# Two linear-attention blocks on one core: the key projection by seven products over pairs of token tiles

## The chip, the core and the metric

The kernel runs as one program on one NeuronCore of a Trainium2 chip. The core has five engines, each with its own instruction queue, worked off in order: TensorE (PE in the profile, with its weight loads as PEld) multiplies matrices into PSUM, VectorE (DVE) and ScalarE (ACT) do elementwise work, GpSimd (POOL) does some elementwise work and issues transfers, and SyncE (SP) issues most transfers. PSUM holds eight banks of 128 x 512 fp32. The metric is device time in microseconds of one execution; lower is better.

## The reference

Two independent blocks A and B have the same shapes: x is 2048 x 640, wqkv 640 x 1920, wo 640 x 640, with 32 heads of 20 columns, all fp32. Each block computes

```
q, k, v = split(x @ wqkv)
phi(t)  = where(t > 0, t + 1, exp(t)) + 1e-6
pq, pk  = phi(q), phi(k)
kv = sum over s of pk[s, d] * v[s, e]        (per head)
z  = sum over s of pk[s, d]
o  = (pq @ kv) / (pq . z + 1e-6)
out = o @ wo
```

and the two outputs stand side by side in a 2048 x 1280 result.

## The kernel before

All matrix products run on values split in two: a rounded high part (ScalarE) and the remainder as a low part (VectorE), both in a 32-bit format that TensorE takes at full rate. A product is then three matmuls: high x high, high x low, low x high (`mm3`, L77).

The first half of the program handles 32 token tiles of 128 rows, 16 of each block, in eight groups of four. For a tile, `kmm` (L200) multiplies the transposed tile by wk: five slices of the inner dimension, three matmuls each, two column halves of 320, so 30 matmuls of 128 x 320 into a pair of PSUM banks. `kphi` (L208) makes phi out of it: Exp and Relu on ScalarE straight from PSUM, a combination on VectorE (L219), the high part on ScalarE (L220), the low part on VectorE (L221); GpSimd adds the unsplit value to a running sum in SBUF by an accumulating transfer (L227). After four tiles, `gmm` (L229) sums x^T times pk over the group: ten blocks of 128 x 320, twelve matmuls each, evacuated by VectorE into a running sum (L263, L265). `gmm` of group i runs after tile 4i+5, so the phi of its last tile has a tile and a half of time. The multiplication by wv and wo is moved to small matrices (`kvmm` L305, `mmm` L327), which for each block give one 640 x 640 matrix md.

The second half handles eight units of 512 tokens: `qmm` (L415) makes q transposed, and `outmm` (L525) multiplies the divided phi(q) by md. `outmm` already uses the seven-product scheme: for a pair of token tiles and md cut into a 2 x 2 grid plus a rest, seven products take 18 terms of three matmuls, 54 in place of 60. It needs sums of the left blocks (`d_sums` L479, `d_split` L496) and ten forms of md, made by VectorE (`form_sums1` L358 and after), split (`form_split` L382), stored in DRAM and loaded again.

No scheduler orders the work. The code is written so that instructions come out in order, and a table of slots (`at`, `run`, L85 to L91) hangs side work on named places: ("k", n, c) after slice c of tile n, ("g", i, s) after block s of group i, ("q", u, c, k) and ("o", u, s) in the second half. A low part waits in a list and comes out at the next slot (`flush`, L66).

## Time and profile before

| | |
|---|---|
| median of 3 runs | 585.66 us (585.63 to 586.2) |
| the profiled execution, its own time | 585.71 us |
| span from first to last instruction | 583.9 us |
| PE busy | 577.9 us, 99% |
| DVE busy | 374.4 us, 64% |
| ACT busy | 289.7 us, 50% |
| POOL busy | 68.7 us, 12% |
| granted TensorE clock | 0.999 |
| moved by DMA | 115.97 MB, 199 GB/s on average |

The span is what the trace covers; 1.8 us of the execution lie outside it. "Busy" of PE counts overlapping matmuls once; a single matmul's duration is longer than its share of the time, since matmuls are pipelined, so the time per matmul is read from the chain of waits (duration of a run of matmuls over their count).

### The profile page before, as it was taken

What the parts mean: (1) busy time and instruction counts of PE and PEld (TensorE: products, weight loads), DVE (VectorE), ACT (ScalarE), POOL (GpSimd) and SP (SyncE); (2) the same over time, 40 slices, a digit from 0 to 9 for tenths busy, and PEclk for the clock granted to TensorE, in tenths of its full rate; (3) what the DMA queues carried; (4) which work ended last, traced back from release to release, by engine and by line L of the source; (5) the groups of instructions that cost most, each with busy time, mean ns of one, the idle gap of its engine ahead of it and who ended that gap; (6) DMA issues with size and microseconds to landing.
All of it is one profiled execution on the core that took longest, in us unless ns stands there. A gap on an engine that the chain in (4) does not pass through costs nothing.

```text
span 583.9 us, 9377 instructions
## 1 busy us (share of the span) xinstructions
PE 577.9 (99%) x3620; PEld 549.6 (94%) x3620; DVE 374.4 (64%) x561; ACT 289.7 (50%) x488; POOL 68.7 (12%) x113
## 2 busy tenths in 40 slices
PE   8999999999999999999999999999999999999997
PEld 6999999999999999999998889898998989898897
DVE  5764573635456357476444599968689775757792
ACT  5752634425056175361525766645747455545541
POOL 0120201100011011232100101211011200001010
PEclk9999999999999999999999999999999999999999
DMA  8986864756667659789899795764183996122022
GB/s 285 274 215 191 230 182 111 183 173 187 167 167 193 193 126 263 253 238 299 230 296 270 252 325 182 267 204 171 46 292 100 382 373 203 77 73 91 2 91 90
DMA packets 66897, 115.97 MB, mean 199 GB/s; under 512 B 6372, under 2 KB 29412, under 8 KB 66852
## 3 DMA queue, kind: packets, MB, share of 16 engines
q1 hardware_dynamic: 56708, 82.92, 44.7%
q0 software_dynamic: 10144, 32.45, 20.0%
q8 instruction: 28, 0.46, 0.3%
q14 instruction: 17, 0.14, 0.1%
HBM read 69.47 MB, written 35.39 MB: 180 GB/s over the span
## 4 chain that ended last, share of the span: by engine, by line
PE 98%; DMA 1%; SPq 0%; DVE 0%; issue 0%; ACT 0%; DVEq 0%
PE psk L196 24%; PE pa L549 12%; PE psg L80 8%; PE psg L79 8%; PE psg L78 8%; PE psq L78 8%; PE psq L80 8%; PE psq L79 8%; PE pe L549 6%; PE psb L549 4%; PE pskv L312 2%; DMA wst<-in_A_wk 1%; PE psm L78 1%; PE psm L80 1%; PE psm L79 1%; PE psd L458 0%
## 5 line engine op out<-in xcount | busy, mean ns | idle before, releaser
L80 PE MATMUL psg<-pkh,xnl 128*128 128x320 f32 x320 | 98.9, 309 | 0.0
L79 PE MATMUL psg<-pkl,xnh 128*128 128x320 f32 x320 | 98.9, 309 | 0.0
L78 PE MATMUL psg<-pkh,xnh 128*128 128x320 f32 x320 | 98.9, 309 | 0.0
L78 PE MATMUL psq<-xqh,wqh 128*128 128x512 f32 x200 | 78.6, 393 | 0.0
L80 PE MATMUL psq<-xqh,wql 128*128 128x512 f32 x200 | 78.0, 390 | 0.0
L79 PE MATMUL psq<-xql,wqh 128*128 128x512 f32 x200 | 77.9, 390 | 0.0
L196 PE MATMUL psk<-wkh,xth 128*128 128x320 f32 x320 | 73.9, 312 | 1.1 <-ACT xth L72 1.1
L196 PE MATMUL psk<-wkh,xtl 128*128 128x320 f32 x320 | 73.3, 310 | 0.2 <-DVE xtl L69 0.2
L196 PE MATMUL psk<-wkl,xth 128*128 128x320 f32 x320 | 73.0, 309 | 0.0
L79 PEld LDWEIGHTS psg<-pkl,xnh 128*128 128x128 f32 x320 | 60.1, 188 | 0.0
L80 PEld LDWEIGHTS psg<-pkh,xnl 128*128 128x128 f32 x320 | 60.1, 188 | 0.0
L78 PEld LDWEIGHTS psg<-pkh,xnh 128*128 128x128 f32 x320 | 60.1, 188 | 0.0
L196 PEld LDWEIGHTS psk<-wkh,xth 128*128 128x128 f32 x320 | 53.5, 189 | 2.1 <-ACT xth L72 1.3
L196 PEld LDWEIGHTS psk<-wkh,xtl 128*128 128x128 f32 x320 | 53.7, 189 | 0.5 <-DVE xtl L69 0.5
L196 PEld LDWEIGHTS psk<-wkl,xth 128*128 128x128 f32 x320 | 53.7, 188 | 0.0
L564 ACT ACTIVATE o<-pa 128x320 f32<-128x320 f32 x64 | 27.9, 438 | 45.5 <-PE pa L549 45.3
L219 DVE SCALAR_TENSOR_TENSOR pk<-ek,rk 128x640 f32<-128x640 f32 x32 | 26.4, 825 | 37.1 <-ACT rk L218 36.7
L265 DVE TENSOR_TENSOR gacc<-psg,gacc 128x320 f32<-128x320 f32 (+1 forms) x59 | 28.5, 493 | 32.3 <-PE psg L80 32.3
L437 DVE SCALAR_TENSOR_TENSOR pq<-eq,rq 128x512 f32<-128x512 f32 x40 | 27.6, 690 | 30.5 <-ACT rq L436 30.5
L227 POOL DMA_DIRECT2D zacc<-pk x30 | 25.6, 853 | 174.6 <-DVE pk L219 120.5
L80 PEld LDWEIGHTS psq<-xqh,wql 128*128 128x128 f32 x200 | 37.5, 188 | 7.9
L221 DVE SCALAR_TENSOR_TENSOR pkl<-pk,pkh 128x640 fp32r<-128x640 f32 x32 | 26.4, 826 | 28.7 <-ACT pkh L220 28.7
(122 smaller groups left out, 1203.2 us busy)
## 6 DMA issues: line engine op xcount, KB each, us to landing
xd<-xtl SPq DMA_DIRECT2D x32, 320.0 KB, 3.7
zacc<-pk POOLq DMA_DIRECT2D x32, 320.0 KB, 4.2
xql<-xd SPq DMA_DIRECT2D x40, 256.0 KB, 4.3
out<-o POOLq DMA_DIRECT2D x28, 320.0 KB, 4.2
xns<-in_A_x SPq DMA_DIRECT2D x16, 320.0 KB, 3.2
xts<-in_B_xt_tiles SPq DMA_DIRECT2D x16, 320.0 KB, 3.4
xns<-in_B_x SPq DMA_DIRECT2D x16, 320.0 KB, 3.3
xqs<-in_A_xt SPq DMA_DIRECT2D x20, 256.0 KB, 5.4
```

The costliest lines, as they stand in the source:

```text
L78: nc.tensor.matmul(o, whi, xhi, start=first, stop=False)
L79: nc.tensor.matmul(o, whi, xlo, start=False, stop=False)
L80: nc.tensor.matmul(o, wlo, xhi, start=False, stop=last)
L196: nc.tensor.matmul(ps[:, h, :HF], a[:, c, :], w[:, h * HF:(h + 1) * HF], start=(c == 0 and i == 0), stop=(c == NC - 1 and i == 2))
L219: nc.vector.scalar_tensor_tensor(p.rearrange("p (a b) -> p a b", a=2), e, 1.0, r, op0=OP.min, op1=OP.add)
L221: nc.vector.scalar_tensor_tensor(lo, p, EPS, f32(hi), op0=OP.add, op1=OP.subtract)
L227: nc.gpsimd.dma_start(zacc[b], p, accum_op=OP.add)
L265: nc.vector.tensor_tensor(o, ps, o, op=OP.add)
L312: nc.tensor.matmul(ps[:r, :r].rearrange("p (d h) -> p d h", h=nh), w[:, c, :], gd, start=(c == 0), stop=(c == NC - 1))
L437: nc.vector.scalar_tensor_tensor(pq[u][:, c, :], e, 1.0, r, op0=OP.min, op1=OP.add)
L549: nc.tensor.matmul(ps, x, y, start=start and n == i == 0, stop=n == len(terms) - 1 and i == 2, skip_group_check=True)
L564: copy = lambda x, y: nc.scalar.activation(x, y, AF.Copy)
```

## The change

**Products.** The first three pairs of token tiles (tiles 0 to 5) are multiplied as before (now in `kconv`). From the fourth pair on, x times wk is done for two tiles at once by the seven products of `outmm`, whose tables and evacuation (`STEPS`, `product`, `combine`) are now shared. Pairs number 3 to 15, thirteen in all. Each product accumulates in one of three banks of its pair ("a", "e", "b"); ScalarE copies bank "a" after products 0, 2, 4 and 5 and VectorE adds banks "b" and "e" into the result in SBUF after products 3, 4 and 6. A product that goes on accumulating in a bank has to wait until the copy of it is done.

**Left and right operands.** `x_parts` splits the blocks of x that are used as they are, `x_sums` makes four sums of blocks on VectorE and splits them. Ten forms of wk are made per block: for A on VectorE, kept in SBUF; for B on GpSimd, stored in DRAM and loaded over A's forms (`wform_load`).

**Order.** `both` interleaves the seven products of two pairs, and blocks of the group sum are put between the products of the second. Groups 3 and 7 have one pair, group 4 has three pairs and block A's `kvmm`. `later` and `tick` spread phi over following slots: Exp and Relu, then the combination, the high part, the low part. Exp and Relu now read SBUF.

**GpSimd and DRAM.** The sums and low parts of the forms of md for both blocks, and the low parts of wo for A, move from VectorE to GpSimd. z is summed in two DRAM tiles per block (odd and even token tiles) by accumulating transfers; they are loaded, added on GpSimd (`z_sum`) and multiplied by ones as before. Only the low parts of x that exist are stored for the second half; the others are made there (`round_xq`).

**PSUM.** One pool serves the whole program: three single banks, two "a", two "e", one small.

```diff
+    def bank(name, tag="one"):
+        return psums.tile([P, 512], F32, name=name, tag=tag, bufs={"one": 3, "a": 2, "e": 2, "small": 1}[tag])
...
+    def split(hi, lo, src, now=False, pool=False):
         nc.scalar.activation(hi, src, AF.Copy)
-        lows.append((lo, src, hi))
-        if now:
-            flush()
+        if pool:
+            nc.gpsimd.tensor_tensor(lo, src, f32(hi), op=OP.subtract)
+        elif now:
+            low(lo, src, hi)
+        else:
+            later(1, low, lo, src, hi)
...
+    def x_parts(p, i):
+        r1, r2 = pair_x(p)
+        hi, lo = (kx[0].tile([P, 4, P], F32R, name=f"ka{t}", tag=f"ka{t}{i}", bufs=2) for t in "hl")
+        ka[p, i] = (hi, lo)
+        if i == 0:
+            split(hi, lo, r1[:, 0:4])
+        else:
+            split(hi[:, 0:3], lo[:, 0:3], r2[:, 2:5])
+            split(hi[:, 3], lo[:, 3], r1[:, 4])
+        later(3, store_xt, p, i)
+    def x_sums(p, i):
+        r1, r2 = pair_x(p)
+        a11, a12, a21, a22 = r1[:, 0:2], r1[:, 2:4], r2[:, 0:2], r2[:, 2:4]
+        tt = nc.vector.tensor_tensor
+        if i == 0:
+            t = ks[p, 2] = kx[0].tile([P, 2, 2, P], F32, name="sx", tag="sx", bufs=2)
+            tt(t[:, 0], a21, a22, op=OP.add)
+            tt(t[:, 1], t[:, 0], a11, op=OP.subtract)
+        else:
+            t = ks.pop((p, 2))
+            tt(t[:, 1], a12, t[:, 1], op=OP.subtract)
+            tt(t[:, 0], a11, a21, op=OP.subtract)
+        hi, lo = (kx[0].tile([P, 2, 2, P], F32R, name=f"ks{t}", tag=f"ks{t}{i}", bufs=2) for t in "hl")
+        ks[p, i] = (hi, lo)
+        flat = "p f c s -> p (f c s)"
+        later(1, split, *(x.rearrange(flat) for x in (hi, lo, t)))
...
+    STEPS = [
+        (ksum(A11, 0, 0), "a", True),
+        (ksum(("s", 0, 0), 0, 1), "e", True),
+        (ksum(("s", 0, 1), 2, 0), "a", False),
+        (ksum(A12, 4, 0) + [(A15, 0, (8, 0))], "b", True),
+        (ksum(("s", 1, 0), 2, 1) + [(A25, 0, (8, 1))], "a", False),
+        ([(A22, k, (6, k)) for k in range(2)] + [(A25, 0, (9, 0))], "a", False),
+        (ksum(("s", 1, 1), 4, 1) + [(A15, 0, (8, 1))], "e", False),
+    ]
...
+        terms, where, start = STEPS[n]
+        o = ps[where]
+        for m, ((kind, i, j), k, w) in enumerate(terms):
+            ah, al = (t[:, j + k] if kind == "a" else t[:, j, k] for t in (asum if kind == "a" else ssum)[i])
+            wh, wl = right(*w)
+            for r, (x, y) in enumerate(((ah, wh), (ah, wl), (al, wh))):
+                nc.tensor.matmul(o, x, y, start=start and m == r == 0,
+                                 stop=m == len(terms) - 1 and r == 2, skip_group_check=True)
...
+        if n == 0:
+            copy(t1[:, 0], ps["a"])
+        elif n == 2:
+            copy(t1[:, 1], ps["a"])
+        elif n == 3:
+            plus(t1[:, 0], ps["b"])
+        elif n == 4:
+            copy(t2[:, 1], ps["a"])
+            plus(t2[:, 1], ps["e"])
+        elif n == 5:
+            copy(t2[:, 0], ps["a"])
+        elif n == 6:
+            plus(t1[:, 1], ps["e"])
...
+    def wform(b, i):
+        w = width(i)
+        wf[b, i] = [kx[0].tile([P, w], F32R, name=f"wf{t}{i}", tag=f"wf{t}{i}", bufs=1) for t in "hl"]
+        return wf[b, i]
...
+    def kprod(p, n):
+        b = p // (NT // 2)
+        def right(i, h):
+            if i == 6 or i == 9:
+                return wf[b, i + h]
+            return [t[:, h * HF:(h + 1) * HF] for t in wf[b, i]]
+        if n == 0:
+            kps[p] = {"a": bank("pa", "a")[:, :HF]}
+            kout(p)
+        elif n == 1:
+            kps[p]["e"] = bank("pe", "e")[:, :HF]
+        elif n == 3:
+            kps[p]["b"] = bank("psb")[:, :HF]
+        product(n, kps[p], [ka[p, i] for i in range(2)], [ks[p, i] for i in range(2)], right)
+        combine(n, kps[p], *ko[p])
+        run("p", p, n)
+        if n > 4:
+            kphi(2 * p + 6 - n, ko[p][6 - n])
...
+    def kphi(n, r):
+        b = n // NT
+        e = kg[0].tile([P, 2, HF], F32, name="ek", tag="ek", bufs=3)
+        hi, lo = pk[n] = [kg[0].tile([P, 2, HF], F32R, name=f"pk{t}", tag=f"pk{t}", bufs=6) for t in "hl"]
+        def mix():
+            nc.vector.scalar_tensor_tensor(e, e, 1.0, r, op0=OP.min, op1=OP.add)
+            z = zacc.get((b, n % 2))
+            if z is None:
+                z = zacc[b, n % 2] = dram.tile([P, D], F32, name=f"zd{b}{n % 2}")
+                nc.gpsimd.dma_start(z, e.rearrange("p a b -> p (a b)"))
+            else:
+                nc.gpsimd.dma_start(z, e.rearrange("p a b -> p (a b)"), accum_op=OP.add)
+            later(1, high)
+        def high():
+            nc.scalar.activation(hi, e, AF.Identity, bias=epst)
+            later(1, lowp)
+        def lowp():
+            nc.vector.scalar_tensor_tensor(lo, e, EPS, f32(hi), op0=OP.add, op1=OP.subtract)
+        def start():
+            nc.scalar.activation(e, r, AF.Exp)
+            nc.scalar.activation(r, r, AF.Relu)
+            later(1, mix)
+        if n % 2 or n in (NT - 2, NN - 2):
+            start()
+        else:
...
+    def load_z(b):
+        for t in range(2):
+            wst["z", b, t] = base.tile([P, D], F32, name="zs", tag=f"wo{'hl'[t]}", bufs=2)
+            nc.sync.dma_start(wst["z", b, t], zacc.pop((b, t)))
+    def z_sum(b):
+        x, y = (wst.pop(("z", b, t)) for t in range(2))
+        nc.gpsimd.tensor_tensor(x, x, y, op=OP.add)
+        wst["z", b] = x
...
+        split(*parts, raw.pop((f, b, i))[:, :w], pool=True)
+        fd[f, b, i] = [dram.tile([P, w], F32, name=f"fd{f}{t}{b}{i}") for t in "hl"]
+        for d, t in zip(fd[f, b, i], parts):
             nc.gpsimd.dma_start(d, f32(t))
...
+    def wform_load(i):
+        for d, t in zip(fd.pop(("k", 1, i)), wform(1, i)):
+            nc.sync.dma_start(f32(t), d)
...
+    forms("k", 1, [(0, ("g", 1, 8)), (2, ("p", 5, 1)), (6, ("p", 6, 2)), (4, ("h", 2, 0)), (1, ("g", 2, 0)),
+                   (3, ("g", 2, 2)), (5, ("g", 2, 4)), (7, ("g", 2, 6)), (8, ("g", 2, 8)), (9, ("p", 7, 5))])
+    for i, a in ((0, ("p", 7, 2)), (1, ("p", 7, 2)), (4, ("h", 3, 2)), (5, ("h", 3, 2)), (8, ("h", 3, 2)),
+                 (2, ("h", 3, 3)), (3, ("h", 3, 3)), (6, ("h", 3, 4)), (7, ("h", 3, 4)), (9, ("g", 3, 3))):
+        at(a, wform_load, i)
...
+    at(("p", 9, 2), load_z, 0)
+    at(("kv", 3), z_sum, 0)
+    at(("g", 4, 2), zmm, 0)
+    at(("q", 0, 0, 0), z_sum, 1)
+    at(("g", LG, 7), load_z, 1)
+    at(("q", 0, 1, 0), zmm, 1)
...
+    def both(p, r):
+        prods(p, 0, 1, 3, 2)
+        prods(r, 0)
+        prods(p, 4)
+        prods(r, 1)
+        prods(p, 5)
+        prods(r, 3)
+        prods(p, 6)
+        prods(r, 2)
...
+    for i in range(NU):
+        P0, P1 = 2 * i + 1, 2 * i + 2
+        if i == 0:
+            gsums(i, range(2 * NC), range(4))
+        elif i in (NG - 1, LG):
+            prods(P0, 0, 1, 3, 2)
+            gsums(i, [0], [0, 1])
+            prods(P0, 4)
+            gsums(i, [1], [0, 1])
+            prods(P0, 5, 6)
+            if i == LG:
+                close_pool(kx, "kx")
+                open_pool(q1a, "q1a", "right")
+                open_pool(q1b, "q1b", "right")
+            gsums(i, range(2, 6), [0, 1], {3: "a", 4: "e", 5: "small"})
+            gsums(i, range(6), [3])
+            gsums(i, range(6), [2])
+            gsums(i, range(6, 2 * NC), range(4))
+        elif i == NG:
+            both(P0 - 1, P0)
+            kvs(0)
+            prods(P0, 4)
+            kvs(1)
+            prods(P0, 5, 6)
+            kvs(2, 3, 4, 5)
+            gsums(i, range(3), [0, 1])
+            gsums(i, range(3), [2, 3])
+            gsums(i, [3], range(4))
+            prods(P1, 0, 1, 3, 2)
+            gsums(i, [4], range(4))
+            prods(P1, 4)
+            gsums(i, [5], range(4))
+            prods(P1, 5, 6)
+            gsums(i, range(6, 2 * NC), range(4))
+        else:
+            both(P0, P1)
+            gsums(i, [0], [0, 1])
+            prods(P1, 4)
+            gsums(i, [1, 2], [0, 1])
+            prods(P1, 5, 6)
+            gsums(i, range(3), [2, 3])
+            gsums(i, range(3, 2 * NC), range(4))
```

Three places in the order of instructions matter to the prediction.

First, ScalarE in the first half, around the phi of a tile. Before, for one tile (xnh is the high part of an x tile, ek and rk are Exp and Relu, pkh the high part of phi):

```order
L72 ACTIVATE xnh_1052<-xns_781 128x640
L217 ACTIVATE ek_1070<-psk_1033 128x640
L218 ACTIVATE rk_1071<-psk_1033 128x640
L220 ACTIVATE pkh_1073<-pk_1072,epst_66 128x640
L72 ACTIVATE xnh_1100<-xns_829 128x640
```

Now, in group 1, where pa_748 and pa_804 are bank "a" of pairs 3 and 4, and ko the result in SBUF:

```order
L262 ACTIVATE ko_750<-pa_748 128x320
L82 ACTIVATE xnh_828<-xn_729 128x640
L262 ACTIVATE ko_750<-pa_748 128x320
L340 ACTIVATE ek_851<-ko_750 128x640
L341 ACTIVATE ko_750<-ko_750 128x640
L333 ACTIVATE pkh_852<-ek_851,epst_66 128x640
L262 ACTIVATE ko_805<-pa_804 128x320
L340 ACTIVATE ek_880<-ko_749 128x640
L341 ACTIVATE ko_749<-ko_749 128x640
L262 ACTIVATE ko_806<-pa_804 128x320
```

The copies of bank "a", which TensorE waits for, stand in the queue between the steps of phi.

Second, VectorE in group 4, at block A's `kvmm` (kvt takes a block out of its PSUM bank). Now:

```order
L265 TENSOR_TENSOR ko_2007<-pe_2036,ko_2007 128x320
L323 SCALAR_TENSOR_TENSOR ek_2175<-ek_2175,ko_2008 128x640
L458 TENSOR_TENSOR kvt_2204<-pskv_2198,mask6_700 120x120
L79 TENSOR_TENSOR ksl_2174<-sx_2170,ksh_2173 128x512
L79 TENSOR_TENSOR kvl_2206<-kvt_2204,kvh_2205 120x120
L458 TENSOR_TENSOR kvt_2222<-pskv_2216,mask6_700 120x120
L337 SCALAR_TENSOR_TENSOR pkl_2177<-ek_2175,pkh_2176 128x640
L323 SCALAR_TENSOR_TENSOR ek_2195<-ek_2195,ko_2007 128x640
L79 TENSOR_TENSOR kvl_2224<-kvt_2222,kvh_2223 120x120
L458 TENSOR_TENSOR kvt_2240<-pskv_2234,mask4_705 80x80
```

Before, the six blocks of `kvmm` were spread over four tiles. Now four of them follow each other, and what empties their banks stands behind two tiles' combination (L323).

Third, SyncE at the end of group 7, where block B's z has to come back from DRAM (zs are the two sums, zd the tiles in DRAM, wv slices of wv). Now:

```order
L199 DMA xql_3770<-xd0_137 128x512
L431 DMA wv_3780<-in_B_wv 128x600
L431 DMA wv_3787<-in_B_wv 128x600
L431 DMA wv_3805<-in_B_wv 128x600
L409 DMA zs_3823<-zd10_2123 128x640
L409 DMA zs_3825<-zd11_2074 128x640
L431 DMA wv_3827<-in_B_wv 128x600
```

Before, this queue held no z, since the sum lay in SBUF. It now stands behind the third slice of wv.

615 lines of the change are left out of this document (300 added, 315 removed), and 4 rows, old and new, of the table LG.

## The prediction

> **What bounds the kernel now.** I read the page's busy times and its chain of waits first, then the chain in order of time, then the groups by shape and single stretches of the timeline.
>
> ```profile
> PE   577.9 (99%) x3620; PEld 549.6 (94%) x3620; DVE 374.4 (64%) x561; ACT 289.7 (50%) x488; POOL 68.7 (12%) x113
> ...
> PE 98%; DMA 1%; SPq 0%; DVE 0%; issue 0%; ACT 0%; DVEq 0%
> ```
>
> TensorE is busy for 99% of the span and makes up 98% of the chain: it waits almost nowhere, so the time is the number of matmuls times what one takes. The chain in order of time (start, length, work, count) gives that price.
>
> ```profile
> 51.35 17.59 PE psk L196 x120
> ...
> 157.82 1.05 PE pskv L312 x10
> ...
> 178.13 0.71 PE pskv L312 x10
> ...
> 301.11 1.01 PE psz L279 x10
> ...
> 348.23 1.76 PE pa L549 x12
> ...
> 353.59 2.63 PE psb L549 x18
> ```
>
> A 128x320 matmul costs 17.59/120 = 146.6 ns in x times wk, and 1.76/12 = 146.7 and 2.63/18 = 146.1 ns in the seven products that the second half already does. The form of product makes no difference to TensorE; only the count does.
>
> **What the change removes.** A pair of tiles took 60 matmuls and takes 54. Thirteen pairs save 78 matmuls, 78 x 0.1466 = 11.4 us. Nothing else on TensorE changes in number. The question is what of it the other engines give back, so the rest of this part goes through the places where TensorE now may wait.
>
> **Load of the helpers in a plain group.** The prices, by shape (busy us, mean ns of one):
>
> ```profile
> L564 ACT ACTIVATE o<-pa 128x320 f32<-128x320 f32 x64 | 27.9, 438 | 45.5 <-PE pa L549 45.3
> L218 ACT ACTIVATE rk<-psk 128x640 f32<-128x640 f32 x32 | 22.4, 699 | 0.0
> L220 ACT ACTIVATE pkh<-pk,epst 128x640 fp32r<-128x640 f32 x32 | 26.6, 831 | 29.0 <-DVE pk L219 29.0
> L72 ACT ACTIVATE xnh<-xns 128x640 fp32r<-128x640 f32 x32 | 23.2, 727 | 23.9 <-PE psg L79 18.2 <-DMA xts<-in_A_xt_tiles 5.5 <-DMA xns<-in_A_x 0.3
> L72 ACT ACTIVATE dsh<-sr 128x512 fp32r<-128x512 f32 x4 | 2.5, 631 | 1.3 <-DVE sr L489 0.8 <-DVE sr L493 0.5
> ...
> L265 DVE TENSOR_TENSOR gacc<-psg,gacc 128x320 f32<-128x320 f32 x58 | 27.7, 487 | 30.0 <-PE psg L80 30.0
> L221 DVE SCALAR_TENSOR_TENSOR pkl<-pk,pkh 128x640 fp32r<-128x640 f32 x32 | 26.4, 826 | 28.7 <-ACT pkh L220 28.7
> L69 DVE TENSOR_TENSOR xnl<-xns,xnh 128x640 fp32r<-128x640 f32 x32 | 26.2, 820 | 9.6 <-ACT xnh L72 9.6
> L69 DVE TENSOR_TENSOR dsl<-sr,dsh 128x512 fp32r<-128x512 f32 x4 | 2.7, 669 | 0.1
> L489 DVE TENSOR_TENSOR sr<-sr,pq 128x256 f32<-128x256 f32 x2 | 0.9, 426 | 0.1
> L317 DVE TENSOR_TENSOR kvt<-pskv,mask 120x120 f32<-120x120 f32 x8 | 2.2, 281 | 7.5 <-PE pskv L312 7.5
> ```
>
> A plain group is two pairs and one group sum, (108 + 120) x 0.1466 = 33.4 us of TensorE. VectorE gets six adds of banks and ten evacuations (16 x 0.487 = 7.8), eight steps of phi (8 x 0.826 = 6.6), four low parts of x (4 x 0.82 = 3.3), eight sums (8 x 0.426 = 3.4) and, per pair, four 512-wide low parts, one of them in two pieces (about 2.8): 26.7 us, 80% of the stretch. ScalarE gets eight copies (3.5), Exp and Relu (8 x 0.70 = 5.6), four high parts of phi (3.3) and of x (2.9) and the pairs' splits (about 5.4): 20.7 us. Before, a group's windows show 9.64 + 9.27 = 18.9 us of VectorE and 13.9 us of ScalarE in 35.3 us:
>
> ```profile
> 33.60:51.20 17.60, 17.60 (x123) 17.60 (x122) 9.64 (x16) 5.60 (x8) 2.50 (x4) 1.00 0.88 221
> 51.20:68.90 17.70, 17.70 (x123) 17.70 (x122) 9.27 (x18) 8.28 (x12) 2.88 (x4) 1.00 0.68 191
> ...
> 283.50:302.00 18.50, 18.50 (x132) 18.50 (x130) 10.41 (x18) 8.22 (x13) 0.94 (x2) 1.00 0.97 280
> ```
>
> Both engines still fit under TensorE; neither becomes the bound on average. What counts is the order inside a group.
>
> **Hand-overs of bank "a".** Product 4 may not start before the copy after product 2 has ended, and only six matmuls (0.88 us) lie between: a copy of 0.44 us fits if ScalarE is free. The tightest point is where the copies stand behind phi. This is how long phi takes when nothing is in its way (start, length):
>
> ```profile
> 17.73 0.68 ACT L217 ACTIVATE ek<-psk 128x640 f32<-128x640 f32 x1
> 18.32 0.70 ACT L218 ACTIVATE rk<-psk 128x640 f32<-128x640 f32 x1
> 19.91 0.83 ACT L220 ACTIVATE pkh<-pk,epst 128x640 fp32r<-128x640 f32 x1 [0.89 <-DVE pk L219]
> 20.64 0.72 ACT L72 ACTIVATE xth<-xts 128x640 fp32r<-128x640 f32 x1
> ...
> 17.35 0.82 DVE L69 TENSOR_TENSOR xtl<-xts,xth 128x640 fp32r<-128x640 f32 x1
> 18.08 0.82 DVE L69 TENSOR_TENSOR xnl<-xns,xnh 128x640 fp32r<-128x640 f32 x1
> 19.05 0.83 DVE L219 SCALAR_TENSOR_TENSOR pk<-ek,rk 128x640 f32<-128x640 f32 x1
> ```
>
> From Exp to the next instruction behind the high part: 20.64 - 17.73 = 2.91 us; an engine passes work on within 0.05 us, and a following instruction starts 0.1 us before the one ahead has ended. In `both`, the queue after product 5 of the first pair is copy, Exp, Relu, high part, copy of the second pair's product 2: about 0.35 + 2.91 + 0.44 = 3.7 us. TensorE has products 3 and 6 (nine matmuls each), product 2 and a partial sum (six each), 30 x 0.1466 = 4.4 us, before it needs that copy. Fits by 0.7 us: cost 0; if ScalarE brings a lag of 1 us along, 0.3 us in each of five places.
>
> In groups 3 and 7 the sums wait for phi of the pair just multiplied. From product 5's end to its low part: 0.35 + 2.91 + 0.83, plus the second tile's Exp and Relu in the queue between, some 5 us; TensorE has nine matmuls and four partial sums, 33 x 0.1466 = 4.8 us. I take 0.1 us each, **0.2** in all (0 to 1).
>
> **First group sum.** In the first six tiles ScalarE gets 48 instructions of 29 us in 26.4 us of TensorE, so it enters the sum late, and VectorE has 17.8 us in a sum of 17.6 us. TensorE is held only when an evacuation is two blocks late (2 x 1.76 us, three banks). **0.3** (0 to 1).
>
> **Group 4.** After product 5 of pair 9, TensorE needs 1.32 us for product 6, 2 x 1.05 + 2 x 0.71 for four blocks of `kvmm` and 0.88 for a partial sum, and at 5.7 us it wants the bank that kvt_2240 empties. On VectorE that stands behind the second tile's combination, which needs Relu, which on ScalarE stands behind copy, Exp, Relu, a split, kvh and the first high part: done at about 5.3 us. Combination, kvl and kvt add 1.3 us: 6.6. TensorE loses **0.9** us (0 to 1.6).
>
> **Forms on GpSimd.** 65 sums and low parts now run there, 31,040 columns in all; the trace has no such instruction. The nearest rows:
>
> ```profile
> L171 POOL IOTA ij<- 128x128 int32 x1 | 0.6, 554 | 0.0
> ...
> fdl<-fsl POOLq DMA_DIRECT2D x14, 320.0 KB, 4.4
> ...
> fh<-fdh SPq DMA_DIRECT2D x14, 320.0 KB, 7.4
> ...
> xqs<-in_A_xt SPq DMA_DIRECT2D x20, 256.0 KB, 5.4
> ```
>
> Bounds for a 640-wide low part: VectorE's 0.82 us, and 640 x 554/128 = 2.8 us. I take 1.8, the middle, since the one row is of another engine and the other of another operation. A form then holds its buffer for 0.73 (ScalarE) + 1.8 + 1.1 (two issues) + 4.4 = 8.0 us, and in group 2 the buffer is wanted again after four blocks, 7.0 us, so ScalarE waits 1 us in each of four forms. It has 11.9 us of work in the 15 us of those sums, so the wait about fills its slack. **0.4** (0 to 3.6). B's forms are loaded after pair 7's product 6 and wanted 17 us later; at the 280 GB/s of the window above 17 us move 4.7 MB, and the forms wanted first with what is between are about 4.6 MB. 0 (0 to 3).
>
> [...]
>
> **z, and the start of the second half.** z adds 32 accumulating transfers to DRAM in place of SBUF; two of one parity are at least 60 matmuls or 8.8 us of TensorE apart, above the 7.4 us of the slowest landing row, so they hide. At the end of group 7 the two loads stand behind a slice of wv that needs a staging buffer whose last reader on VectorE stands behind six evacuations and five low parts (6 x 0.487 + 5 x 0.82 = 7.0 us). Counted from the end of block 6: buffer free at 3.1, loads issued at 4.1, landed (4.4 to 5.4) at 8.5 to 9.5, summed on GpSimd at 10.3 to 11.3; `zmm` is due after three blocks and about 5.2 us of q, at 10.5. **0.5** (0 to 3).
>
> Start (first stall below) and second half: the same loads in the same order, the same matmuls, 0.
>
> ```profile
> 8.37 0.55 PE L196 MATMUL psk<-wkh,xth 128*128 128x320 f32 x2 [1.07 <-ACT xth L72]
> ```
>
> **Sum.** Span 583.9 - 11.4 + 0.2 + 0.3 + 0.9 + 0.4 + 0.5 = 574.8 us; with the 1.8 us outside the span (585.71 - 583.9) **576.6 us**. The profiled execution lies 0.05 us from the median of 585.66, so I make no correction.
>
> **Rivals.** *GpSimd holds up VectorE.* If an engine's arithmetic blocked the other's while it runs, the most loaded group (2) would have 26.7 - 7.8 (work on PSUM) + 6080 columns x 1.8/640 = 36.0 us against 33.4, 2.6 us over, and the first unit of the second half about 1 us: 576.6 + 3.6 = 580.2 us. For it: nothing in this trace, where GpSimd does no arithmetic. Against it: elsewhere VectorE has 20% free. [...]
>
> *Late data at the two seams.* Block B's forms of wk and z each come 2 to 3 us late because the queues are fuller than their median landing says (97% DMA share in the last window quoted): 576.6 + 5.4 = 582 us. Against it: both have some slack by the rows.
>
> *ScalarE late at every hand-over.* In five interleaved pairs of pairs three hand-overs have only 0.88 us, in three single pairs two: 21. If Exp and Relu stand ahead of the copy, it comes 1.40 + 0.44 - 0.88 = 0.96 us late, 21 x 0.96 = 20 us: 597 us, slower. The change breaks even at 11.4/21 = 0.54 us per hand-over. For it: the copies do share the queue with phi. Against it: the walk above leaves 0.7 us.
>
> **Chances.** The forecast has 0.70 (its own range 574.3 to 579.5, all terms at zero to terms at about twice their size), GpSimd holding up VectorE 0.09, late data 0.09, the hand-overs 0.12, of which 0.08 past break-even. That gives 0.88 for faster by over 0.2%, 0.04 for within 0.2% (a difference that a measurement here can't tell from none) and 0.08 for slower. The range of 574.2 to 583.0 us holds the forecast and both rivals of the middle.
>
> **What would show it.** Right: 3472 matmuls from the core of the program at 146.6 ns in the chain, PE's idle time a few us above before, most of it in group 4, in the first group sum and at the first products of the second half. A stall at kvt in group 4 of some 0.9 us checks that walk. GpSimd's 640-wide sums show their price; VectorE's 820 ns grown in the stretches where GpSimd works would show the exclusion. Waits of "pa" on the copies in every group would show the hand-overs. The forecast is wrong if TensorE's idle time in the first half is over 8 us, or if a matmul costs other than 146.6 ns.

## The result: slower by 4.3%, and the profile after

The changed kernel takes **611.14 us** (median of four executions, 609.68 to 611.92) against 585.75 us before: 1.0429 times as long, interval 1.0409 to 1.0449. Forecast were 576.6 us, range 574.2 to 583.0. The profiled execution has a span of 609.2 us, 25.3 us longer than before and 34.4 us longer than forecast. Of the experiments below, one execution of run 1 (938.3 us) and one of run 7 (598.3 us) were disturbed and are left out of the times, the traces of these two runs come from them and are not read here, and the expectations that name 593.6 and 590.8 us still include them.

Busy times and the chain of waits of the changed kernel's page:

```profile
PE 581.4 (95%) x3542; PEld 545.5 (90%) x3542; DVE 454.2 (75%) x681; ACT 336.6 (55%) x615; POOL 170.4 (28%) x204
...
PE 57%; DVE 15%; issue 8%; ACT 8%; DMA 7%; POOL 4%; SPq 1%; POOLq 0%; DVEq 0%; ACTq 0%
```

The saving is there: 3542 matmuls instead of 3620. But TensorE is now idle for 609.2 - 581.4 = 27.8 us of the span (6.0 before), and its busy time rose in spite of 78 matmuls fewer. In the chain it fell from 98% to 57%: VectorE, ScalarE, GpSimd and transfers now stand in the chain beside it. VectorE's busy time rose by 80 us (374.4 before). The waits of TensorE (who for whom, us in total, times, longest):

```profile
PE pa L258 <- ACT ko L262: 7.9, 11, 2.5
PE psg L91 <- DVE gacc L399: 6.2, 4, 2.2
PE psg L91 <- DVE kvt L458: 2.7, 2, 1.5
PE psk L363 <- ACT kah L82: 2.2, 1, 2.2
PE psz L420 <- POOL zs L413: 1.8, 1, 1.8
```

Stages of the first half, by windows from one stage's first matmul to the next one's (TensorE, weight loads, VectorE, ScalarE, GpSimd, granted clock, DMA share, GB/s):

```profile
52.90:88.20 35.30, 33.75 (x231) 33.49 (x230) 26.46 (x46) 19.53 (x35) 7.83 (x8) 1.00 0.62 140
88.20:128.80 40.60, 36.38 (x230) 34.95 (x230) 33.30 (x45) 22.55 (x39) 28.89 (x32) 0.96 0.87 250
...
255.20:294.60 39.40, 36.01 (x230) 34.95 (x229) 33.79 (x42) 21.97 (x38) 32.42 (x37) 0.96 0.86 259
```

These are groups 1, 2 and 6, each with the same work on TensorE, 33.4 us. Group 1, with 7.8 us of GpSimd, takes 35.3 us, and VectorE's 26.46 us are close to the 26.7 us of the prediction (in part by chance, since the last instructions of this group are already lengthened beside GpSimd's first sums). Groups 2 and 6, with about 30 us of GpSimd, take 40.6 and 39.4 us. VectorE has no more instructions there (45 and 42 against 46) and is busy 7 us longer. The groups by shape of the changed kernel say which instructions grew (busy us, mean ns of one). Here fsl is the low part of a form, pkl that of phi(pk) and xnl that of an x tile, pq is phi(q) and gacc the running group sum; further down, kal and ksl are the low parts of blocks of x and of their sums sx, and kah and ksh the high parts:

```profile
L84 POOL TENSOR_TENSOR fsl<-wst,fsh 128x640 fp32r<-128x640 f32 x15 | 27.0, 1802 | 27.6 <-ACT fsh L82 22.8 <-DMA fdml<-fsl 3.7 <-DMA fdkl<-fsl 1.1
...
L337 DVE SCALAR_TENSOR_TENSOR pkl<-ek,pkh 128x640 fp32r<-128x640 f32 x32 | 32.8, 1024 | 7.0 <-ACT pkh L333 6.2
L574 DVE SCALAR_TENSOR_TENSOR pq<-eq,rq 128x512 f32<-128x512 f32 x40 | 31.5, 788 | 27.7 <-ACT rq L573 27.6
L79 DVE TENSOR_TENSOR xnl<-xn,xnh 128x640 fp32r<-128x640 f32 x32 | 28.7, 922 | 6.2 <-ACT xnh L82 5.6
L399 DVE TENSOR_TENSOR gacc<-psg,gacc 128x320 f32<-128x320 f32 x60 | 27.7, 482 | 8.1 <-PE psg L93 8.0
```

The mean of pkl went from 826 to 1024 ns, of xnl from 820 to 922, of pq from 690 to 788; gacc, which takes one operand from PSUM, stayed at 482 (487 before). One stretch of the timeline shows what a mean hides, and how it reaches TensorE (start, length, engine, work, idle time before and who ended it):

```profile
130.72 2.11 DVE L79 TENSOR_TENSOR kal<-xt,kah 128x384 fp32r<-128x384 f32 x2
130.79 1.89 POOL L84 TENSOR_TENSOR fsl<-wst,fsh 128x640 fp32r<-128x640 f32 x1 [1.23 <-ACT fsh L82]
...
133.09 0.41 DVE L165 TENSOR_TENSOR sx<-xt 128x256 f32<-128x256 f32 x1
...
133.53 0.63 ACT L82 ACTIVATE ksh<-sx 128x512 fp32r<-128x512 f32 x1 [2.83 <-DVE sx L165]
134.07 0.42 ACT L262 ACTIVATE ko<-pa 128x320 f32<-128x320 f32 x1
```

TensorE's rows of that stretch:

```profile
131.69 0.31 PE L258 MATMUL psb<-wfh,kal 128*128 128x320 f32 x1
134.54 0.41 PE L258 MATMUL pa<-wfh,ksh 128*128 128x320 f32 x1 [2.54 <-ACT ko L262]
134.79 0.31 PE L258 MATMUL pa<-wfl,ksh 128*128 128x320 f32 x1
```

Read from the top of the first of the two. VectorE's two low parts (0.75 us where nothing disturbs them) last until GpSimd's subtraction has ended, 2.11 us. The sum sx behind them is late by that. ScalarE stands before ksh, which rounds sx, for 2.83 us. Behind ksh in ScalarE's queue is the copy that empties bank "a", whose product had long been done; TensorE waits for that copy, 2.54 us. From the start of the last matmul ahead of the wait to the start of the second one behind it lie 134.79 - 131.69 = 3.10 us, where two matmuls take 0.29. So this wait costs some 0.27 us more than its idle time of 2.54 us, and the other waits between two matmuls of this shape cost 0.26 to 0.32 us more.

Last, the granted clock in three windows of 3.41 us (length, TensorE, clock, DMA share, GB/s):

```profile
118.04:121.45 3.41, 1.64 (x11) 1.00 0.99 259
121.45:124.86 3.41, 3.41 (x15) 0.50 0.86 267
124.86:128.28 3.42, 2.77 (x19) 1.00 0.72 228
```

After a wait TensorE ran for one such window at exactly half clock. There are five of them (at 121.5, 135.1, 186.3, 288.7 and 329.7 us), each 1.7 us lost at most; before, there was none ahead of the tail.

A matmul at full clock costs what it did; the chain in order of time has

```profile
56.17 3.08 PE pa L258 x21
```

which is 146.7 ns for one.

The account of the 25.3 us: -11.4 (matmuls) + 21.8 (idle, 27.8 - 6.0) + about 7.7 (half clock: some 1.5 us in each of five windows, where a 128x320 matmul takes 267 ns) + about 6.5 (0.27 us at 24 waits more than before) = 24.6.

### The profile page after: what moved, and what is told of

It reads as the page before. It is cut to its first block, busy times and chain, and to the rows that moved or that the text cites. A ratio compares the mean times of both kernels' runs of the same rounds, so it can differ in the third digit from the quotient of the medians.

```text
span 609.2 us, 9675 instructions
## 1 busy us (share of the span) xinstructions
PE 581.4 (95%) x3542; PEld 545.5 (90%) x3542; DVE 454.2 (75%) x681; ACT 336.6 (55%) x615; POOL 170.4 (28%) x204
## 4 chain that ended last, share of the span: by engine, by line
PE 57%; DVE 15%; issue 8%; ACT 8%; DMA 7%; POOL 4%; SPq 1%; POOLq 0%; DVEq 0%; ACTq 0%
PE pa L258 15%; PE psq L91 6%; PE psq L92 6%; PE psq L93 6%; PE pe L258 6%; PE psb L258 5%; PE psg L91 3%; PE psg L93 3%; PE psg L92 3%; DVE kal L79 2%; DVE ek L323 2%; ACT ko L341 2%; ACT ek L340 2%; POOL fsl L84 1%; PE psk L363 1%
## 5 line engine op out<-in xcount | busy, mean ns | idle before, releaser
L329 POOL DMA_DIRECT2D zd<-ek x28 | 24.9, 889 | 85.9 <-DVE ek L323 74.2
L572 ACT ACTIVATE eq<-psq 128x512 f32<-128x512 f32 x40 | 23.8, 596 | 37.1 <-PE psq L93 32.0
L82 ACT ACTIVATE ksh<-sx 128x512 fp32r<-128x512 f32 x26 | 16.4, 630 | 50.6 <-DVE sx L161 25.7
L91 PEld LDWEIGHTS psq<-xqh,wqh 128*128 128x128 f32 x200 | 37.9, 189 | 7.2
L92 PEld LDWEIGHTS psq<-xql,wqh 128*128 128x128 f32 x200 | 37.9, 189 | 7.2
L693 POOL DMA_DIRECT2D out<-o x14 | 7.6, 539 | 123.2 <-ACT o L262 123.2
L262 ACT ACTIVATE ko<-pa 128x320 f32<-128x320 f32 x52 | 22.4, 430 | 34.6 <-PE pa L258 34.4
L79 DVE TENSOR_TENSOR kal<-xt,kah 128x128 fp32r<-128x128 f32 (+2 forms) x49 | 34.8, 736 | 4.8 <-ACT kah L82 4.8
L337 DVE SCALAR_TENSOR_TENSOR pkl<-ek,pkh 128x640 fp32r<-128x640 f32 x32 | 32.8, 1024 | 7.0 <-ACT pkh L333 6.2
L323 DVE SCALAR_TENSOR_TENSOR ek<-ek,ko 128x640 f32<-128x640 f32 x32 | 28.4, 889 | 11.3 <-ACT ko L341 11.3
```

Of the source, the lines that this page charges most:

```text
L79: nc.vector.tensor_tensor(lo, src, f32(hi), op=OP.subtract)
L82: nc.scalar.activation(hi, src, AF.Copy)
L91: nc.tensor.matmul(o, whi, xhi, start=first, stop=False)
L92: nc.tensor.matmul(o, whi, xlo, start=False, stop=False)
L262: nc.scalar.activation(x, y, AF.Copy)
L323: nc.vector.scalar_tensor_tensor(e, e, 1.0, r, op0=OP.min, op1=OP.add)
```

## The experiments

Ratios are to the kernel before, measured on the same chip, with the 95% interval.

**1. GpSimd's arithmetic on VectorE.**

```diff
-        split(*parts, raw.pop((f, b, i))[:, :w], pool=True)
+        src = raw.pop((f, b, i))[:, :w]
+        nc.scalar.activation(parts[0], src, AF.Copy)
...
+            low(parts[1], src, parts[0])
...
+        later(1, rest)
...
-        tt = (nc.gpsimd if pool else nc.vector).tensor_tensor
+        tt = nc.vector.tensor_tensor
```

> The 65 additions and subtractions that the changed kernel gives to GpSimd (91.4 us of its time) are given to VectorE instead; GpSimd keeps its DMA issues. In the trace of the change 98 VectorE instructions that overlap a GpSimd addition take 49 us longer than the same instructions elsewhere; here they would take their own 38 us or so in its place, in fixed places of VectorE's queue. Theory 1 (GpSimd's arithmetic holds VectorE up, the late sums hold ScalarE's queue up, and the copies that empty bank a behind them hold TensorE up; a TensorE that stood idle then runs some us at half clock): no VectorE instruction is longer than its kind elsewhere, TensorE's waits fall from 29 us to 8 to 15 us, the stretches at half clock from 5 to 0 to 3, and the time is 586 to 600 us, 592 as the likeliest. Rival theory 2 (the hand-over of bank a is too tight by itself, whoever makes the forms): waits stay near 29 us and the time is above 604 us. Rival theory 3 (VectorE has no room for the forms): the lengthening is gone, VectorE is busy over 95% in the stages with forms, and the time is 600 us or more.

593.0 us, 1.0126 (1.0109 to 1.0143): 18 us less than the change, as theory 1 said. Theory 2 (the hand-over is too tight whoever makes the forms) and theory 3 (VectorE has no room) would have left the time above 604 us and at 600 us or more, and fall. VectorE is given 65 more instructions than in the change, and the kernel is faster.

**2. That arithmetic left out.**

```diff
-        split(*parts, raw.pop((f, b, i))[:, :w], pool=True)
+        nc.scalar.activation(parts[0], raw.pop((f, b, i))[:, :w], AF.Copy)
...
-        for d, t in zip(fd[f, b, i], parts):
+        for d, t in zip(fd[f, b, i], (parts[0], parts[0])):
```

> Those 65 additions and subtractions are left out altogether: the low parts that they made are replaced by the high parts, the sums by one of the summands, and z's two halves are not added, so the output is not the reference's. Loads, stores, ScalarE's roundings and GpSimd's DMA issues stay. Theory 1: no VectorE instruction is longer than its kind elsewhere, of TensorE's 29 us of waits there are left the start-up (3.5), the waits for kvt (3.0 or less), part of the wait for z and a few of under 0.5 us, some 10 us in all; at most two stretches at half clock; 580 to 588 us, 583 as the likeliest. Theory 2: waits for the copies out of bank a stay, 600 us or more.

585.0 us, 0.9991 (0.9967 to 1.0014). The sums and z's addition are left out in the same way, so the output is not the reference's. 26 us of the loss go with the arithmetic, while the forms' loads and stores stay. Yet 8 us over the forecast stay. The waits of this run:

```profile
PE pa L258 <- ACT ko L262: 4.1, 6, 2.3
...
PE psg L91 <- DVE kvt L457: 1.2, 1, 1.2
PE psk L363 <- ACT kah L82: 0.8, 1, 0.8
```

The longest one, 2.3 us, has the same form as the one above with another cause, a load that landed late; in the timeline of this run:

```profile
95.34 0.74 ACT L82 ACTIVATE xnh<-xn 128x640 fp32r<-128x640 f32 x1 [3.72 <-DMA xn<-in_A_x]
...
99.57 0.42 ACT L262 ACTIVATE ko<-pa 128x320 f32<-128x320 f32 x1
```

ScalarE stood 3.72 us before the rounding of a slice of x, and phi and the copies out of bank "a" behind it came late by that.

**3. GpSimd's arithmetic alone, in the kernel before.**

```diff
         pk[n] = (hi, lo)
+        nc.gpsimd.tensor_tensor(e, e, e, op=OP.subtract)
```

> The kernel before, with one subtraction of 128x640 on GpSimd behind each tile of phi(pk), 32 in all, on a buffer that nobody reads any more (the result is not used). Theory 1 in its two halves: VectorE's instructions with both operands in SBUF that overlap them take up to 1 us longer (20 us or more in all), and the time stays within 1.5 us of the kernel before, since there no bank of PSUM waits for VectorE in less than the 17.6 us of a group; so the lengthening costs only where TensorE waits on VectorE soon. If it is the lengthening in itself that counts, TensorE stands idle here too and the time is 590 us or more.

587.35 us, 1.0025 (1.0011 to 1.0038). The timeline of this run:

```profile
128.08 0.83 ACT L220 ACTIVATE pkh<-pk,epst 128x640 fp32r<-128x640 f32 x1 [0.89 <-DVE pk L219]
128.14 1.24 POOL L223 TENSOR_TENSOR ek<-ek 128x640 f32<-128x640 f32 x1 [19.95 <-DVE pk L219]
128.94 1.12 DVE L221 SCALAR_TENSOR_TENSOR pkl<-pk,pkh 128x640 fp32r<-128x640 f32 x1 [0.90 <-ACT pkh L220]
```

and its groups by shape:

```profile
L221 DVE SCALAR_TENSOR_TENSOR pkl<-pk,pkh 128x640 fp32r<-128x640 f32 x32 | 35.9, 1120 | 28.7 <-ACT pkh L220 28.7
```

The exclusion, VectorE waiting for GpSimd's arithmetic, shows by itself: pkl, begun at 128.94, ends at 130.06, which is GpSimd's end (129.38) plus 0.68; the mean of the 32 rose from 826 to 1120 ns. That is 9.4 us of VectorE and not the 20 us expected, since GpSimd began when VectorE was idle; and TensorE waited once more, 0.4 us. The same lengthening that costs little here costs much where a bank is wanted back in 0.88 us.

**4. B's z later.**

```diff
-    at(("q", 0, 0, 0), z_sum, 1)
-    at(("q", 0, 1, 0), zmm, 1)
+    at(("q", 0, 1, 0), z_sum, 1)
+    at(("q", 0, 2, 0), zmm, 1)
```

> The changed kernel with the sum of z's two halves of B and its ten matmuls put some 3.5 us (one block of 15 matmuls of xq x wq) later; nothing else. The trace of the change shows TensorE idle 1.84 us there and a stretch of 3.4 us at half clock right after. Expected if both belong to that wait: 3.0 to 4.0 us less, 607.5 us. If the stretch at half clock is not the wait's doing: 2 us less. If the second half's loss lies elsewhere: the same as the change.

606.0 us, 1.0343 (1.0328 to 1.0359), 5.1 us less than the change. In the trace the wait for z and the half clock behind it are gone (3.4 us in the second half); the rest is mostly a start 1.2 us shorter, which differs from run to run.

**5. Wider hand-overs, forms still on GpSimd.**

```diff
-        prods(r, 0)
-        prods(p, 4)
-        prods(r, 1)
-        prods(p, 5)
-        prods(r, 3)
-        prods(p, 6)
-        prods(r, 2)
+        prods(r, 0, 1)
+        prods(p, 4)
+        prods(r, 3)
+        prods(p, 5)
+        prods(r, 2)
+        prods(p, 6)
```

> The changed kernel with another order of the products where two pairs are interleaved: p0 p1 p3 p2, r0 r1, p4, r3, p5, r2, p6 in place of p0 p1 p3 p2, r0, p4, r1, p5, r3, p6, r2, so that 1.76, 1.32 and 1.32 us of matmuls lie between a product and the next one on the same bank a where it was 0.88 us; arithmetic on GpSimd as in the change. Theory 1 (GpSimd's arithmetic is the cause; the hand-over only passes the lateness on): the short waits for the copies (0.3 to 0.6 us each, 2 to 3 us in all) go, the long ones shrink by 0.4 to 0.9 us each; 605 to 609 us, 607 as the likeliest. Theory 2 (the hand-over's 0.88 us is itself the cause): the 9.2 us of waits for copies go, and the half clock with them; below 600 us.

610.8 us, 1.0423 (1.0403 to 1.0443): no gain. The waits for copies fell from 7.9 to 6.7 us, but the first pair's last product and its phi now come later, and the group sums waited 3.3 us for phi's low part where it was 0.3. The hand-over's 0.88 us is not the cause; and neither theory had the new wait.

**6. Forms on VectorE, z later and wider hand-overs together** (the edits of 1, 4 and 5).

> Three edits together: GpSimd's 65 additions on VectorE, z of B later, and the wider hand-overs. If the three losses are separate, they add: 593.6 us less 3.5 us for z (the addition itself is now on VectorE) less 2 to 3 us for the hand-overs, 587 to 588 us, range 585 to 590. If the wider hand-overs and the forms on VectorE mend the same waits: 590 to 592 us.

592.4 us, 1.0120 (1.0095 to 1.0144). The gains don't add. In this run VectorE's instructions have their old length (groups by shape; xnl is at 819 ns again and pq at 691), and the second view is what TensorE still waits for:

```profile
L337 DVE SCALAR_TENSOR_TENSOR pkl<-ek,pkh 128x640 fp32r<-128x640 f32 x32 | 26.3, 822 | 6.0 <-ACT pkh L333 5.6
```

```profile
PE pa L258 <- ACT ko L262: 2.9, 4, 1.0
PE psg L92 <- DVE pkl L337: 2.9, 3, 2.0
PE psg L91 <- DVE kvt L458: 2.2, 1, 2.2
PE psg L91 <- DVE gacc L399: 1.6, 1, 1.6
```

What TensorE waits for is again an instruction of VectorE, or of ScalarE behind VectorE; the forms now stand in VectorE's own queue.

**7. Blocks of gacc x wv spread.**

```diff
-            kvs(2, 3, 4, 5)
-            gsums(i, range(3), [0, 1])
+            kvs(2, 3)
+            gsums(i, [0], [0, 1], {0: "a"})
+            kvs(4)
+            gsums(i, [1], [0, 1], {1: "e"})
+            kvs(5)
+            gsums(i, [2], [0, 1])
```

> As the three together, and the six blocks of gacc x wv no longer three or four behind each other but with a half group sum (0.88 us) between the last ones, so that VectorE has emptied a bank before the next sum needs it. The trace of the change shows 3.0 us of waits for kvt there and a stretch at half clock. Expected: 1.4 to 3.5 us less than the three together, 585 us, range 582.5 to 587.5. If the wait is only moved: no difference.

590.2 us, 1.0067 (1.0045 to 1.0090): 2.2 us less than run 6, as expected in size, from a higher start.

**8. Seven products for A alone.**

```diff
-            both(P0, P1)
+            if i < NG:
+                both(P0, P1)
+            else:
+                plain(P0)
+                plain(P1)
```

Here `plain` does a pair with 60 matmuls from B's raw wk, split into high and low part.

> As the run before it, but with seven products only for A's five pairs and the plain product for B's eight pairs, so that no forms of B's wk are made, stored or loaded, and no sums of B's token tiles. TensorE has 48 matmuls more (7.0 us at 146.6 ns). If B's forms and B's tight hand-overs cost less than 7.0 us beside what is mended already: slower than the run before it, 588 to 592 us. If they cost more (the sum of the waits in groups 2 to 6 of the change says 15 us): 581 to 584.5 us, faster than the kernel before too, whose 585.7 us it would undercut by up to 4.4 us (30 matmuls fewer).

590.45 us, 1.0082 (1.0052 to 1.0113), the same as run 7. The 7.0 us of TensorE that B's eight pairs save are given back in full.

**9. Free forms, mended order** (run 2 with the edits of 5 and 7).

> As the run without the 65 additions (so the output is not the reference's: forms rounded from raw weights, z from one half), with the wider hand-overs and the spread gacc x wv. It shows what the seven products would give if the forms' arithmetic cost nothing on any engine. The forecast of the prediction without its terms for forms and kvt is 575.3 us. If the 10 us that TensorE still waited without the arithmetic are hand-overs and kvt: 578 to 581 us. If they are late loads and VectorE's other work: within 2 us of the run without the additions, 583 to 587 us.

582.7 us, 0.9947 (0.9934 to 0.9960), no half clock; this lies between the two expectations. Even with forms that cost no arithmetic, the seven products would win 3 us and not 11; the rest stands in many short waits, behind the start none over 0.7 us:

```profile
PE pa L258 <- ACT ko L262: 1.3, 3, 0.7
...
PE psg L92 <- DVE pkl L337: 0.9, 2, 0.5
PE psg L91 <- ACT pkh L333: 0.8, 2, 0.5
```

**10. A alone, mended.** Against run 8:

```diff
-            gsums(i, range(6), [3])
-            gsums(i, range(6), [2])
+            for j in ((2, 3) if i == LG else (3, 2)):
+                gsums(i, range(6), [j])
...
-    at(("h", 6, 1), form_sums2, "m", 0, 1)
+    at(("g", 6, 2), form_sums2, "m", 0, 1)
...
+                    nc.scalar.activation(e[:, h], two[h], AF.Exp)
+                    nc.scalar.activation(r[:, h], two[h], AF.Relu)
```

> Seven products for A alone, as measured at 590.45 us (profile 586.3 us of span), with what its trace shows TensorE waiting for put elsewhere: forms of M after the group sums' additions in VectorE's queue instead of before them (1.94 us at 259.9 us), the last group's sums of tile 30 before those of tile 31 (1.33 us at 288 us), the sums of the next token tiles one group sum later in the first group (0.43 us), Exp and Relu of B's tiles straight from PSUM (ScalarE 0.74 us less a tile). Expected if these waits go and none comes: span 582.5 to 583.5 us, time 584.0 to 586.0 us, 585 as the likeliest, and no half clock. If another wait takes their place: 588 to 590 us.

585.82 us, 1.0004 (0.9985 to 1.0024). The time is as expected, but half clock did not go from all executions. They lie between 584.1 us (clock 1.000) and 588.7 us (0.994), so how much half clock the waits bring differs from one to the next; two windows of it explain 3 of these 4.6 us.

**11. Both batches, forms put behind the group sums' additions** (run 7 with moved slots of `forms`, `form_sums2` and `form_last` for wk and M, and the first group's parts and sums of x one block later).

> Seven products for both batches with the forms on VectorE, z later, wider hand-overs and spread gacc x wv (590.76 us measured), and the forms of wk and of M put after the group sums' additions in VectorE's queue, the first group's fills one sum later. If the place in VectorE's queue is what makes TensorE wait (3.5 us at 264 us, 1.4 at 122 us and some half clock in the profile of that run): 585 to 588 us. If VectorE is simply late in these groups: no change, 590 to 592 us.

591.15 us, 1.0097 (1.0083 to 1.0111): no change. The waits moved (gacc 1.4, copies 3.3, xnl 1.3 us) and did not go. That fits the second expectation, that VectorE is late in these groups wherever the forms stand; only this one other order was tried.

**12. A alone, the start of the second half.** B's first parts of wo are split later, M's first block with them; z is added on GpSimd, and the x of groups 3 and 7 is split one product earlier:

```diff
-        at(("q", 0, 1 + g, 1) if g < 4 else ("q", 1, 0, 2 * g - 7), split_o, 1, g)
+        at((("q", 0, 2, 1), ("q", 0, 2, 4), ("q", 0, 3, 1), ("q", 0, 4, 1), ("q", 1, 0, 1), ("q", 1, 0, 3))[g], split_o, 1, g)
...
+            if q in (7, 15):
+                xs = [("p", q, k) for k in (0, 1, 3, 4)]
```

> As the run of seven products for A alone with its order mended (585.82 us; TensorE reaches the second half at 297.7 us, 4.3 us before the kernel before, and loses it there again: 1.5 us at a bank that VectorE empties late, because in its queue a low part of wo stands ahead whose load lands late, and a stretch at half clock behind it). B's first two parts of wo are split 2.5 to 3.5 us later, M's first block with them; z's halves are added on GpSimd again, where VectorE has room; the token tiles of groups 3 and 7 are split one product earlier. Expected if these are what the second half loses: 582 to 584 us, 583 as the likeliest, faster than the kernel before by 0.3 to 0.6%, and no run at half clock. If the seam is short of DMA: another load is late in its place, 585 to 587 us.

585.06 us, 0.9992 (0.9983 to 1.0001), without half clock ahead of the tail, but not within the 582 to 584 us expected. Behind the start one long wait was left, 1.4 us for a low part of wo.

**13. Stops of known length in the kernel before.**

```diff
+    def stop_pe(k):
...
+        nc.tensor.matmul(ps[:64, :64], pad, pad, start=True, stop=True)
+        nc.scalar.activation(pad[:64], ps[:64, :64], AF.Copy)
+        for _ in range(k - 1):
+            nc.scalar.activation(pad[:64], pad[:64], AF.Copy)
+        nc.tensor.matmul(ps[:64, :64], pad, pad, start=True, stop=True)
```

> The kernel before with 13 stops of TensorE: a tiny matmul, a chain of 3 to 10 small copies on ScalarE, a tiny matmul that waits for them; seven in the group sums 1 to 7 (4 to 10 copies) and six in the second half. They are to last 1.0 to 2.7 us. In the traces so far a stretch of 3.41 us at half clock follows a wait of 1.7 us or more, and none follows one of 1.6 us or less; the stretches begin at whole multiples of 3.41 us from each other. If the wait decides it: half clock after the stops above 1.7 us (about half of them, fewer where the stop lies across a multiple of 3.41 us), none after the shorter ones, and the time is 585.7 us plus the stops' 20 to 25 us plus 1.7 us for each stretch, 612 to 622 us. If half clock comes from the load on the other engines or the memory instead: no stretch at half clock here, since those are as in the kernel before.

631.9 us in the only execution; the stops lasted 0.88 to 2.89 us, 23.8 us in all. Windows along the 3.41 us grid (TensorE, clock, DMA share, GB/s), for stops of 1.46, 1.74, 2.03 and 2.32 us:

```profile
117.86:121.27 3.41, 1.95 (x14) 1.00 0.68 196
121.27:124.68 3.41, 3.41 (x25) 1.00 0.02 5
155.41:158.82 3.41, 1.67 (x13) 1.00 0.69 197
158.82:162.23 3.41, 3.41 (x15) 0.50 0.00 0
203.19:206.60 3.41, 1.40 (x10) 1.00 0.66 193
206.60:210.01 3.41, 3.39 (x13) 0.50 0.23 86
244.16:247.57 3.41, 2.59 (x18) 1.00 0.78 237
247.57:250.98 3.41, 1.91 (x13) 1.00 0.89 271
250.98:254.39 3.41, 3.41 (x25) 1.00 0.41 143
```

Stops of 1.74 and 2.03 us inside one window are followed by a window at half clock. The 1.46 us stop is not, and neither is the one of 2.32 us, which a window's edge cuts into 0.82 and 1.50. Ahead of the tail, all seven windows at full clock with 1.74 us or more of idle time were followed by half clock, and none with 1.50 us or less (one of the seven stretches, behind the stop at 365.0 us, lasted two windows). The time is longer than expected because each stop also costs 0.6 to 0.7 us for its tiny matmuls, 8 us in all. So the half clock of the change belongs to its waits, as run 4 shows for one of them. The bound of 1.7 us for the wait itself, which the expectation takes from earlier traces, does not hold for all of them: in run 10 half clock begins during a wait of 1.6 us.

**14. A alone, the last wait.** M's first two blocks of B 1.8 to 2.1 us later (the third part of wo and the stores of M move with them):

```diff
-        at((("q", 0, 2, 4), ("q", 0, 3, 2), ("q", 0, 4, 4), ("q", 0, 4, 4), ("q", 1, 1, 2), ("q", 1, 2, 2))[g], mmm, 1, g)
+        at((("q", 0, 3, 1), ("q", 0, 4, 0), ("q", 0, 4, 4), ("q", 0, 4, 4), ("q", 1, 1, 2), ("q", 1, 2, 2))[g], mmm, 1, g)
```

> As the run before it of seven products for A alone (585.06 us, span 583.3 us), whose trace shows one wait of 1.6 us left at the start of the second half: the second block of M waits for the low part of wo, which VectorE makes behind the first sums of phi(pq). B's first two blocks of M move 1.8 to 2.1 us later, the third part of wo with them. Expected if that is the last of what the second half gave back of A's 4.4 us: span 581.5 to 582.0 us, time 583.3 to 583.8 us, faster than the kernel before by 0.3%. If the start of the second half takes the gain in any case (its loads land 7.9 us after their issue at the median): 584.7 to 585.5 us.

**583.92 us, 0.9971 (0.9961 to 0.9982)**: faster than both kernels, by 0.3% than the one before, and 0.1 us above what was expected. Its busy times, and the two longest waits after TensorE's first instruction:

```profile
PE 575.3 (99%) x3590; PEld 545.3 (94%) x3590; DVE 408.2 (70%) x666; ACT 316.1 (54%) x602; POOL 76.1 (13%) x121
```

```profile
PE psk L376 <- ACT kah L82: 0.5, 1, 0.5
PE psq L92 <- DMA xql<-xd: 0.4, 1, 0.4
```

TensorE is at 99% again, and no wait is above 0.5 us. Of A's 30 x 0.1466 = 4.4 us the span keeps 1.8 (582.1 against 583.9).

## Why the prediction was wrong

The steps from forecast to measurement; the time in a row is that of the run that still has the losses named down to this row:

| step | time, us |
|---|---|
| forecast | 576.6 |
| short waits at copies, phi and low parts, forms free (run 9) | 582.7 |
| close hand-overs and bunched gacc x wv (run 2) | 585.0 |
| the forms' arithmetic, on VectorE (run 1) | 593.0 |
| the same on GpSimd instead (the change) | 611.1 |

**The step that failed** is the load of the helpers together with the price of the first rival. The forecast let VectorE's 26.7 of 33.4 us stand when 65 additions came to GpSimd, because nothing in the trace of before showed an exclusion. The rival named the mechanism and priced it by average load, 36.0 us for group 2 and 580.2 us in all; group 2 took 40.6 us. The mechanism was right; the price was one of the wrong kind. The exclusion hits single instructions: counted over all rows, 101 of VectorE's overlap a GpSimd addition. The 73 with both inputs in SBUF are 48 us longer than the same instructions elsewhere, and the other 28 keep their length (run 1's expectation, by another count, names 98 and 49 us). What a late one costs is set by what stands behind it in VectorE's queue, then in ScalarE's, and by how soon TensorE wants its bank. In the kernel before that is 1.5 us for 9.4 us of lengthening (run 3); here it is 18 us for 48 (change against run 1), although run 1 puts the additions' own time on VectorE.

The traces show which instructions wait: pkl, kal, sx and xnl last past GpSimd's end (kal by 0.15 us in the rows above, pkl by 0.68 us in run 3), and gacc, with an operand in PSUM, stays at 482 ns. The rival's sum leaves VectorE's 7.8 us of work on PSUM out of the exclusion; no run showed that term when the forecast was made, and what the change shows in its place is gacc's 482 ns and the 28 instructions that keep their length. Its chance of 0.09 was the author's estimate from a trace in which GpSimd does no arithmetic; run 3 is the test that could have settled it.

Point by point:

- **78 matmuls at 146.6 ns**: right: 146.7 ns, and 78 records fewer (3542 in the trace; the prediction's 3472 "from the core of the program" does not say which it leaves out).
- **Hand-overs of bank "a", cost 0**: wrong, 7.9 us of idle in 11 waits. The walk ("fits by 0.7 us") counted what ScalarE has to do before the copy, and not that an instruction ahead of it may itself wait for VectorE (2.83 us above) or for a load (3.72 us in run 2). The rival that priced the hand-overs at 20 us had the place and not the cause: wider ones gained nothing clear of the noise (0.3 us, run 5).
- **Group sums** were in the forecast only with 0.2 and 0.3 us, for phi and the first sum, and those two measured 0.3 + 0.2 and 0.3 us of idle. The 6.2 us of waits for gacc in groups 1, 2 and 6, where an evacuation stands behind a lengthened sx or kal, were not in it.
- **kvt in group 4, 0.9**: right for the wait that it walked through, but 2.7 us came in two waits and a window of half clock. The wait at 183.5 us is the one of the walk: 1.2 us, as in run 2, where GpSimd adds nothing. The second, 1.5 us at 186.1 us, was not foreseen and is the exclusion: VectorE's kvl ahead of it took 2.16 us, beside the addition of A's z on GpSimd, where the other three of its shape take 0.24 us (rows below). Spreading the blocks brings 2.2 us (run 7).
- **Forms on GpSimd, 0.4**: the price of 1.8 us per 640 columns was met (1802 ns), in part by luck, since this mean contains GpSimd's own waiting: the shortest of these 15 take 1.55 to 1.58 us, the longest 2.47. The effect looked for, ScalarE waiting for a form's buffer, came four times and cost TensorE 0.3 us once (at 272.9 us); the effect that mattered was the exclusion.
- **B's forms, 0**: right; nothing waits for them.
- **z, 0.5**: mis-sized, 1.8 us idle and a window of half clock, 3.4 us (run 4). The addition took 1.53 us, but the walk had it end just in time, so a small lateness of the loads counts in full.
- **Start, 0**: the wait for kah was 2.2 us against 1.07; in runs 2, 4, 6, 8, 9, 11, 12 and 14, with the same start, it lay between 0.5 and 1.2 us, so it is spread and not the change's doing.
- **Half clock**: not in the forecast at all, about 7.7 us.

The two rows behind the second wait for kvt:

```profile
183.77 2.16 DVE L79 TENSOR_TENSOR kvl<-kvt,kvh 80x80 fp32r<-80x80 f32 x1 [0.34 <-ACT kvh L82]
183.98 1.85 POOL L413 TENSOR_TENSOR zs<-zs 128x640 f32<-128x640 f32 x1
```

What the prediction said would refute it, over 8 us of TensorE idle in the first half, is what came: 22.1 us.

Not settled: how much of the 18 us between the change and run 1 is VectorE's waiting and how much GpSimd's own (its additions are lengthened too, a form's from 1.55 us up to 2.47, and its stores stand behind them). Both go away together. In the change's timeline nine of TensorE's waits, 13.7 of 24.3 us, have a lengthened VectorE instruction ahead of them in the queues.

## What to carry to other kernels

Work that is moved to an engine because that engine is idle must be asked what it shares with the busy ones: here VectorE's instructions with both inputs in SBUF waited until GpSimd's addition was done (48 us longer in all, for 73 of them), and the same additions on the loaded VectorE cost 18 us less. Price such a lateness along the queues and not by the average: find the urgent instruction (a copy that gives a bank back) and ask what can stand ahead of it waiting for something else. And where a change saves 0.88 us of TensorE per pair of tiles, a single wait of that length per pair undoes it; take such a saving only where the helpers have room, as for A here.
